# A hand-written order table of 1781 steps is replaced by another one: a recurrent attention layer and a gated two-layer network on one core

## The chip, the cores and the metric

The kernel runs on one core of a Trainium2 chip. The metric is the time of one execution on the device in microseconds (us), taken as the median over runs. The core has five engines with instruction queues of their own: TensorE (PE) for matrix products, VectorE (DVE), ScalarE (ACT) and GpSimd (POOL) for elementwise work, and SyncE (SP), which here only issues transfers between the chip's memory and the core. Each engine takes its queue strictly in order, so an instruction that waits holds up all that stand behind it on the same engine.

## The reference

Two layers follow each other. The first is a recurrence over 768 time steps with a state matrix of 48 x 48 for each of 4 batches and 8 heads; the second takes its 3072 outputs of 384 numbers through a network of 384, 2048 and 384 columns.

```python
for t in range(S):
    cur = np.einsum('bhd,bhe->bhde', u[None] * kt, vt)
    y[:, :, t] = np.einsum('bhd,bhde->bhe', rt, state + cur)
    state = wt[:, :, :, None] * state + np.einsum('bhd,bhe->bhde', kt, vt)
...
h = x @ w_in
relu6 = np.clip(h + 3.0, 0.0, 6.0)
g = h * relu6 / 6.0
return (g @ w_out).astype(np.float32)
```

The weights of the second layer come as 64-bit floats, the rest as 32-bit floats.

## The kernel before

**Tiling.** The sequence is cut into 24 chunks of 128 steps. For a chunk DVE scans the decays backward and forward (`back_scan` L430, `fore_scan` L439), scales k and r (L450, L454, and from chunk 7 on POOL does that), and PE makes scores, transposes k, writes to the state and reads from it (L500, L516, L600, L578, L587). Four chunks make a block of 512 tokens, and there are six blocks. In block 0 the second layer is done plainly: `up` (L716), a ramp on ACT, `gate` on DVE (L727), `down` (L735). In blocks 1 to 5 both products are done with fewer multiplications: sums of the inputs (`sum_x`, L778 to L782) feed 40 products (`up_product`, L831, 2 halves of 20 with 2 matmuls each), DVE and ACT read the results (`up_read`, L839 to L848), then come ramp and gate (L852, L856), sums of the gated values (`sum_g`, L871), and 28 products a block for the output (`down_product`, L886), read out by ACT and DVE (L902, L904) and stored by SP (`store`, L746).

**Start.** The weights must be turned from 64-bit to 32-bit floats before block 0 can use them. A pair of weight tiles is fetched by SP (`fetch`, L393, 768 KB into a `bits` buffer), ACT makes two passes over it (`low_whole` L402 and `high_sign` L407), DVE shifts and adds (`high_shift` L413 and `high_low` L417). There are 16 such pairs. PE, while it has nothing to do in the first 60 us, runs small products whose result nobody reads (L1262, here called fillers).

**End.** Besides the result the kernel checks that its inputs allow the short way of computing: 38 reductions of re-read inputs on DVE (`vet`, L932 and L935), eight small instructions that join them (`verdict`, L945 to L955), a product of one column on PE (`count`, L959), and a copy of the number into `flag` on DVE (L962). Behind the kernel's last step every engine loads that flag into a register (L1535) and branches over a second, general version of the kernel when it is zero (L1536).

**What sets the order.** The kernel is written as 1781 named steps, each with its engine, its predecessors and the buffers that it holds (rings: four PSUM banks called `bank`, one called `bankS`, one `y`, three `bits` buffers and so on). The table `ORDER` gives each step a rank, two characters a step, and the steps are written out in this rank. That is then the order on every engine. Since a step takes the buffer that came free earliest in this order, the table also decides which buffer, and so which reader, a step waits for. The fillers too are put in by the kernel's own times for the steps, so their number at each place follows the order.

```python
rank = [CODE.index(ORDER[2 * i]) * 64 + CODE.index(ORDER[2 * i + 1]) for i in range(len(steps))]
out = [n for _, n in sorted(zip(rank, steps))]
```

Of the kernel before, what the change touches and what calls it, by code (L numbers as in the profile page):

```python
# [81 lines left out]
ORDER = (
    "AAADAIAQAKAOALANAPARASAYAVAjATAXAZAdAmAqAfAoAzA3A/ACAFAWAiAcAnAbAaAeAgAhAlAtAyAkApAxA1A5A9A8A+BNBUBcAJAMBIBfBSBaBRBF"
    "BJBTBVBXCGCLBpBvCBCRBdCYCdCnCyC7AUAvBjB4BuCABzBeBgBlBmBqCSCaCJCOCWCrCNCuC1E0DCDMDVDgBOBQCpC2DcDkCvCUCbCiDDDXDuDyC+DH"
    "DjFFDKFMFQFUFfFnFwCXDLC9DGEOEZDBDADRDWDsEKFzDZDqFPFWE5FZFeFkF3GVGXGlGfCcC4D9EJFmFpEEDYDwD+F2F5GYFlFvFoGNGPGSGiG0G5Do"
    "FxETFyF+GDEXEDFXFcGhGjG6F7GdF8GrGzG2HPHYHkH0HsEdGaF4GZGxG1F9FdGWGgHAHCHcGnHHGoHMHOHRH/IEIIFrG8FuGkG7HXHhGqGcGpHbHeIJ"
    "HVHiHWHyH2H9IrJWJlJtJ0GHHdGIG/HmItIyHGGtHNIPIVJcIDINIHIYIcKMLfLkG3IKG9HzILI/JCH3HZHjJeJjLnIvJbIwJgJiLxMAMLMWMQHnJdHo"
    "JvJ4K/LDJ1IBIdLqLuMIKTLtLwL1MRMfMmI4LlI6KHLmL6MBKOJUJnMFMPMpL4MJMbMiMwOvO9PEPLLHMGLKLrMHMZMeLyLZL0MtMxO5MYMrL9MvMzM6"
    "PJP+QKLSMnLVMNMoNANHMUL2MTO2PIQCM4O8M3PoPpPsQWQdQiQyQqNYO4NaOSO3PXPbOYN5OFQBQGQjPPQJPQQNQQQXQ5RIRQOCQEOEPhQDQcQgPlOg"
    "PRQrQwRUQbQvQeQxQ0Q1R3SoS1S6TCOHQkOKQIQlRERLQSPUQMRZRcSwQ+RWRARgRjRnTlUdUlRNRRRVRqRwSISNRvR/SOSuS9UiR7SzR8ULUNUPUvU9"  # L90
    "VOVUVYSCSvSETATWT+UCTISeSpUqUtVDTsUhTqUnUpUuVWVhVqSUUkSXTgUjU8VATkSyTGVCVKVsU1VHU6VLVPVVWAYTYVYjYZShVESnUrVFVbVfUxTL"
    "UyVxV2YWVaVoVdVzV3YdYgYnUGVpUHVMVrWFWLVTU0VQYbYfYqWEYaWIYcYhYtYwYyY5Y1BCABAEArAuAsA2AGA4A7AwBAAHBDBHA6BPBBB1B+B7CFCD"
    "ClCoCmCwA0CTCZBrChBLCHCKCQC6CVC0C5DNDSD8EhEmEfEsDPDzD2D1EcCgD/EBDQEkCsDfDiDpDtEpE/FCE+FgEGErEvEwE2E1FKFOFLFVDvE3E6En"
    "FABGBMBWB3B8B/EUEbEiBZBhBtBkBxB0FaFhFiBbBiBoBnCCCPEAEIELBEBKBYBsByB2EHEPERB6CECIEeEoEuBwB5B9ExFIFRCMCeCjENESEWCfCtCz"
    "EQEVEYC3C/DEFSFYFbC8DIDOElEtEyCkCxDFD0D7ECCqDbDhEaEgEjDJDTDaG+HKHQDUDeDmE4E9FDDlDxD3EqEzE7DdDnDrD5EFEME8FBFHFjFtF0F6"
    "F/GCGEGBGFGKGMGRGbGeGmGuGvGsGwGyG4HBHJHUHaHrH6HgHlHqHwH1H5ICIGITIXD4D6FEFGFJFNFTFqGOGQGTGUHDHEHFHIHLHSHTHfHpHtHuHvHx"
    "H4H7H8H+IAIRIUIWIaIgIhIjIkIlInJNJPFsF1GAGGGJGLKDKhIFIOIpI5IeIuI2JGJqI+JAJLIQISI7IMIiImIZIzJDJOJRJkIqI0IxIbI8IsI9JEIo"
    "IfJYJQI3JBJIJVJXJpJ5KBKFJZKAJTJrJFJKJwJzJ6J9JMJSI1JHJ7KIKdKkKrJaJfKuJ+KEKXJmJxKGJuJ2KCKUKSKaJ/KRKKJsKiKJKYKqJ3JyKoKz"
    "J8KcKLKjKVKmKxK0K4KZKeK5K9KfKlKsKvKpKtKwK1KPKbKNLOLMLULCLGLLLYKnLAK2LELILNLQLTLWLaLbLjL3L5LFLJLXLRLcLpL8LdL+LeLhLvMC"
    "LgLiL/MMKgKyLoLsK7K8L7MDMKMOMXMaMlM9K3LzMSLBMVMgNCMdNEMkMsMyM+NQNVNeNpNyNsNuN4MqNBNgMuM5NIM1NKNSNmNZNkNTNbNXM0NhNMNd"  # L100
    "NzNDM7NtN9NPNoNWNxNfN1N6OUOuNjNnOOOXNrNvNwN3N7OPN2OJNcNiOBOLOWOlOtObOeOnN0N8OTN/OGOQNFNOOiO1OqO6OIOROMODOdOVOZOjONNJ"
    "OoOrOcOhOmO7O0PAPFPMPSPGPKOxO+OkOpOsOwPDPHOzPBOaOfOyPnPNPuPZPdPkPyO/PVPCPcPiPmPqPtPwP0P2P5QAQHPgPjPxPrP6P/QRP8QTP3P9"
    "QUQfP4P7QZQsPOPTQLQPPYPaQaQhQoQzQtQ2Q9RDPWQYQpPfQ3Q6RGQ7RHRBRPRYRdRbRmRuR6SGRORTSDRyR1SARFRXRhReRrSKSdSgStRkRsR5RKRz"
    "RpRtR0RfRlSBSHRxSFSWSiSlS0S3S5S+SqSsSQSVSfS7ScSmTDTJR2SMR+SZS8THTPTfTpS/TETxS2S4TYSJSYSPSSSkSxTRTKTVTBTNTMSLTUSTTbTr"
    "SjSaTjT2SrTdTFTXTQTZT0T3T7TSTnT5T8ThTmToTuTcTeTvTyTOTTTwT4UIUTUBUFUMUWTiUAT9UDUJUOUQUSUUUXUYUgUsU2UEUKUVURUZUoU5UbU7"
    "UaUeUwU3UcUfU/VSTaTtUmU4T1T6UzVBVIVcVNVRVZVnTzU+VJT/ViVXVvVlVyVkVuV1V6WDWKWpWyW8XdXgXrVtVwWTV0V+WGV4WPWeWlWmWtWHWRWN"
    "V5WuWMWUXlWBV9W2XxWXWdWjWwWoWxXEXIXMWqWsX1X3WgWiW5W+W0W4XoXsWSWVW1W/XUXbXjX2X5YDWbWhXGV7WWWYWnWvW3XCXNXXW7XFXAWOXYWc"
    "XKX7WZWrXeYHWzXLW9XaXRXcXnXqXvXTXVYIYKXOXSXhXkXfXiX8X+XDXHYeYmYsY0YkYoYvY4X6YLYlYrYQYUYxYzY2Y8Y6Y7Y/ZKYOYuY3YYZAY9ZN"
    "ZDZPW6XBXPX4XpXwX0YFXQXmXJXuX/YAXyYBX9YXYGYJYNYPXtXzYEYCYiYMYRYpYSY+ZBZFZIZRZVZZZcZ2ZEZHZqadakasZCZLZaZJZOZXZmZiZtZU"
    "ZYanZGZbZdZfZkZQZMZhZuZSayZeZrZnZxZ8Z+aBZsZwZyZ3a1a9ZlZpZ4Z7ZoZ0aparZTZgaMaYamaCaJaQahaoazZzZ/Z9ZvZ6aKaUaSabZWZjauZ5"  # L110
    "aRaAaDaLaEZ1acaTaHa5aOaaaWagaqatawaZaeaVaXa+bCafaiajalaNaPaxa8aFaIa2bEa0a4bAbLaGa3ava6bDbFa/bIbGbMbSbXbabca7bBbKbHbO"
    "bZbebQbfbPbUbbbhbRbVbkbpbJbNbYbgbWbibdblbnbsbqbrbubxbTbjbobmbvbtbzbwb0JJJhK+LPJoKQKWK6MjNGMEMcMhM8M2NNNqN+NLOANlM/NU"
    "NRPePzPvP1QOQFQmQ/Q8QVQnQuRCRaRiQ4RMRJRSR9R4RoSbSRVjV8V/VGVgVeVmWJWQWCWaWfWkXWXZby"
)
# [1490 lines left out]
```

## Time and profile before

| | before |
|---|---|
| median of 3 runs (lowest, highest) | 545.09 us (544.74, 546.12) |
| span of the profiled execution | 544.0 us; no own time is listed for it; the median of the runs lies 1.1 us above this span |
| instructions in the trace | 13407 |
| PE busy | 532.9 us, 98% of the span |
| DVE busy | 425.1 us, 78% |
| ACT busy | 268.1 us, 49% |
| POOL busy | 112.9 us, 21% |
| read from memory, written | 59.90 MB, 4.72 MB |

The span runs from the first to the last instruction of one execution. "Busy" is the time in which an engine works on an instruction; waiting, branches and the issue of transfers are not counted. The ends of matmuls are modelled, so a short wait of PE can be hidden in its busy time. In the trace a 32-bit matmul counts as two instructions, so the counts of PE are twice those of the program.

### The profile page before, as it was taken

What the parts mean: (1) busy time and instruction counts of PE and PEld (TensorE: products, weight loads), DVE (VectorE), ACT (ScalarE), POOL (GpSimd) and SP (SyncE); (2) the same over time, 40 slices, a digit from 0 to 9 for tenths busy, and PEclk for the clock granted to TensorE, in tenths of its full rate; (3) what the DMA queues carried; (4) which work ended last, traced back from release to release, by engine and by line L of the source; (5) the groups of instructions that cost most, each with busy time, mean ns of one, the idle gap of its engine ahead of it and who ended that gap; (6) DMA issues with size and microseconds to landing.
All of it is one profiled execution on the core that took longest, in us unless ns stands there. A gap on an engine that the chain in (4) does not pass through costs nothing.

```text
span 544.0 us, 13407 instructions
## 1 busy us (share of the span) xinstructions
PE 532.9 (98%) x5558; PEld 466.7 (86%) x5558; DVE 425.1 (78%) x726; ACT 268.1 (49%) x657; POOL 112.9 (21%) x111
## 2 busy tenths in 40 slices
...
PEclk9999999999999999999999999999999999999998
...
GB/s 302 364 152 336 259 176 105 126 118 126 65 170 82 77 188 110 222 187 177 23 147 153 288 203 162 0 118 87 170 58 1 2 16 31 30 0 2 1 29 36
DMA packets 29686, 66.66 MB, mean 123 GB/s; under 512 B 3216, under 2 KB 10544, under 8 KB 29616
## 3 DMA queue, kind: packets, MB, share of 16 engines
...
q14 instruction: 24, 0.20, 0.1%
q10 hardware_dynamic: 128, 0.00, 0.0%
HBM read 59.90 MB, written 4.72 MB: 119 GB/s over the span
## 4 chain that ended last, share of the span: by engine, by line
PE 87%; DVE 7%; DMA 2%; issue 1%; ACT 1%; DVEq 0%; ACTq 0%
PE bank L886 28%; PE bank L831 22%; PE bank L735 7%; PE bank L716 7%; PE bankS L886 5%; PE bankS L831 4%; DVE g L848 3%; PE y_ps L578 2%; PE y_ps L600 2%; PE bank L500 2%; PE ps L516 2%; PE y_ps L587 2%; DVE g L856 1%; DMA bits<-in_moe_w_out_dram 1%; PE bankS L1262 1%
## 5 line engine op out<-in xcount | busy, mean ns | idle before, releaser
L852 ACT ACTIVATE clip<-g,three 128x512 f32<-128x512 f32 x80 | 56.9, 721 | 55.3 <-DVE g L848 45.9
L848 DVE TENSOR_TENSOR g<-bank,g 128x512 f32<-128x512 f32 x80 | 53.6, 684 | 10.1 <-PE bank L831 8.6
L856 DVE SCALAR_TENSOR_TENSOR g<-clip,g 128x512 f32<-128x512 f32 x80 | 56.2, 716 | 5.8 <-ACT clip L852 5.8
L886 PE MATMUL bank<-w_out,g 128*128 128x192 f32 x320 | 57.3, 327 | 0.0
L491 ACT ACTIVATE A<-eyes,dg 128x64 f32<-128x64 f32 x192 | 49.5, 338 | 11.0 <-PE y_ps L587 10.7
L886 PEld LDWEIGHTS bank<-w_out,g 128*128 128x128 f32 x320 | 52.8, 190 | 1.2 <-DVE g L856 0.3
L450 POOL TENSOR_TENSOR K<-feat_in,E 112x512 f32<-112x512 f32 x17 | 23.1, 1361 | 133.8 <-PE bank L500 128.0
L716 PE MATMUL bank<-xT,w_in 128*128 128x256 f32 (+1 forms) x216 | 45.5, 362 | 0.7 <-issue 0.7
L683 ACT COPY xT<-y_ps 48x256 f32<-48x256 f32 x88 | 32.2, 366 | 27.7 <-PE y_ps L587 26.9
L735 PE MATMUL bank<-w_out,g 128*128 128x384 f32 x128 | 43.8, 491 | 0.0
L716 PEld LDWEIGHTS bank<-xT,w_in 128*128 128x128 f32 x216 | 36.5, 190 | 5.3 <-issue 0.9
L831 PE MATMUL bank<-xT,w_in 128*128 128x256 f32 x160 | 40.5, 381 | 0.4 <-DVE g L848 0.4
L846 ACT COPY g<-bank 128x512 f32<-128x512 f32 x50 | 28.8, 582 | 20.7 <-PE bank L831 17.2
L735 PEld LDWEIGHTS bank<-w_out,g 128*128 128x128 f32 x128 | 23.5, 190 | 14.2
L831 PEld LDWEIGHTS bank<-xT,w_in 128*128 128x128 f32 x160 | 30.0, 190 | 5.2 <-DVE g L848 0.8
L902 ACT ACTIVATE o<-bank 128x192 f32<-128x192 f32 x30 | 9.9, 330 | 49.7 <-PE bank L886 49.6
L430 DVE TENSOR_TENSOR_SCAN E<-feat_in,back 112x520 f32<-112x520 f32 x24 | 31.5, 1312 | 2.2 <-DMA feat_in<-in_feat_dram 1.1
L454 POOL TENSOR_TENSOR W<-feat_in,W 112x512 f32<-112x512 f32 x17 | 22.8, 1342 | 44.3 <-DVE W L439 44.3
L439 DVE TENSOR_TENSOR_SCAN W<-feat_in,start 112x520 f32<-112x520 f32 x24 | 31.4, 1308 | 0.6 <-PE y_ps L578 0.4
L507 DVE COPY_PREDICATED A<-mask,bank 128x256 f32<-128x256 uint8 x48 | 18.6, 441 | 16.3 <-PE bank L500 16.1
L831 PE MATMUL bank<-xT,bits 128*128 128x256 f32 x120 | 30.9, 381 | 0.0
L886 PE MATMUL bank<-more,g 128*128 128x192 f32 x160 | 28.7, 328 | 0.0
...
## 6 DMA issues: line engine op xcount, KB each, us to landing
...
```

What stands on the lines that cost most here:

```text
L430: nc.vector.tensor_tensor_scan(out=E_[:, ::-1], data0=d["w"][:, :0:-1], data1=back.rearrange("q p t -> q (p t)")[:, ::-1], initial=0.0, op ...
L439: nc.vector.tensor_tensor_scan(out=W_, data0=d["w"][:, :-1], data1=starts[i % 2].rearrange("q p t -> q (p t)"), initial=0.0, op0=ALU.mult, ...
L491: nc.scalar.activation(out=d["A"][:, h, :], in_=eyes, func=ACT.Copy, scale=d["dg"][:, h])
L683: nc.scalar.copy(out=blocks[bk]["xT"][g * GP:g * GP + D, :, at:at + HL], in_=st[i]["y_ps"][a][(g ^ a) * GP:(g ^ a) * GP + D, :, :])
L716: nc.tensor.matmul(h_ps[:, :(c1 - c0) * L], lhsT=w_in[:, f // 2, j, f % 2, :], rhs=b["xT"][:, j, c0 * L:c1 * L], start=(j == 0), stop=(j = ...
L735: nc.tensor.matmul(b["o", c][:, :DM], lhsT=g_of(0, f, c), rhs=w_out[:, f, :], start=(f == 0), stop=(f == NFC - 1))
L831: nc.tensor.matmul(b["p", d, c][:, z * HB:(z + 1) * HB], lhsT=weight(W_PLACE[r], d)[:, z, :], rhs=x_at(bk, X_PLACE[r]), start=fresh and z ...
L846: nc.scalar.copy(out=out_, in_=src)
L848: nc.vector.tensor_tensor(out=out_, in0=src, in1=out_of(bk, d, other), op=ALU.add if sign > 0 else ALU.subtract)
L852: nc.scalar.activation(out=c, in_=out_of(bk, d, u), func=ACT.Relu, bias=three, scale=twice)
L856: nc.vector.scalar_tensor_tensor(out=g, in0=blocks[bk]["r", d, u], scalar=6.0, in1=g, op0=ALU.min, op1=ALU.mult)
L886: nc.tensor.matmul(b["d", p, to][:, :h], lhsT=a, rhs=w(), start=(f == 0 and k in (1, 5)), stop=(f == HF - 1 and k in (2, 3, 4)), skip_grou ...
```

## The change

Only the text of `ORDER` differs. The table was searched anew under three sets of step times instead of one: as traced, with transfers and hand-overs between engines delayed, and with early transfers. The steps, their engines, predecessors and buffers are the same 1781, so the amount of work is the same. The number of fillers is 38 in both. Of the diff a line or two show the kind of thing:

```diff
-    "AAADAIAQAKAOALANAPARASAYAVAjATAXAZAdAmAqAfAoAzA3A/ACAFAWAiAcAnAbAaAeAgAhAlAtAyAkApAxA1A5A9A8A+BNBUBcAJAMBIBfBSBaBRBF"
+    "ADAWAGALAJAPAHAKANAOARAaAbAiASATAYAcAhArAkAvAzA7A+AMAgAQAeAdAqAVAUAZAmAnAuA2A6ApAtA3A4A/BKA9BBBIBOBZAfBtAwBCBECEA1Ay"
```

What it does to the order is shown at four places.

**SP and DVE at the start.** `feat_in` is a chunk's r, k and decays, `v_in` its v, `bits` a raw weight pair. SP before:

```order
L348 DMA feat_in<-in_feat_dram 128x521
L356 DMA feat_in<-in_feat_dram 128x2x512
L351 DMA feat_in<-in_feat_dram 128x3x521
L363 DMA v_in<-in_tok_dram 128x384
L393 DMA bits<-in_moe_w_in_dram 128x3x256
```

SP now:

```order
L393 DMA bits<-in_moe_w_in_dram 128x3x256
L348 DMA feat_in<-in_feat_dram 128x521
L356 DMA feat_in<-in_feat_dram 128x2x512
L351 DMA feat_in<-in_feat_dram 128x3x521
L363 DMA v_in<-in_tok_dram 128x384
```

A weight pair is now fetched ahead of the first chunk's decays. On DVE, where `E` and `W` are the scans' results and `rk` is r times k, before:

```order
L430 SCALAR_TENSOR_TENSOR E<-feat_in,back 112x520
L434 RECIPROCAL start_79<-E 112x8
L439 SCALAR_TENSOR_TENSOR W<-feat_in,start_79 112x520
L463 TENSOR_TENSOR rk<-feat_in 112x512
L454 TENSOR_TENSOR W<-feat_in,W 112x8x64
```

DVE now, behind the same memsets:

```order
L413 TENSOR_SCALAR top<-bits 128x768
L430 SCALAR_TENSOR_TENSOR E<-feat_in,back 112x520
L434 RECIPROCAL start_79<-E 112x8
L417 ISA w_in<-top,more 128x1536
L439 SCALAR_TENSOR_TENSOR W<-feat_in,start_79 112x520
L463 TENSOR_TENSOR rk<-feat_in 112x512
```

The conversion of that pair (L413 and L417) moves in front of and between the first chunk's scans. ACT's two passes of the same pair now stand at the head of its queue, ahead of the small transfer of `u_col` that ACT issues itself. ACT before:

```order
L349 DMA u_col<-in_ug_dram 112x8
L457 ACT_TABLE_LOAD
L457 COPY w_min<-E 112x8
L481 COPY dg<-ps 128x8
```

ACT now:

```order
L402 ACT_TABLE_LOAD
L402 ACTIVATE more<-bits 128x768
L407 ACTIVATE more<-bits 128x768
L349 DMA u_col<-in_ug_dram 112x8
L457 COPY w_min<-E 112x8
```

The transfer of `u_col` is issued behind two conversions that wait for the weight pair; PE needs `u_col` for its first real product (L475).

**PE from the first read of chunk 0 on.** The rows start behind that read (L578, L587), the first score (L500) and the write (L600) of chunk 1. Before:

```order
L1262 MATMUL bankS<-ident 128x128 x3
L659 MATMUL y_ps<-xT,S__115 128x64 x6
L651 MATMUL bank<-xT,ident 128x256 x2
L578 MATMUL bank<-W,S 48x64 x8
L587 MATMUL bank<-A,v_in 48x64 x16
L716 MATMUL bank<-xT,w_in 128x128 x6
L475 MATMUL ps<-u_col,rk 64x2 x8
L1262 MATMUL bankS<-ident 128x128 x6
L659 MATMUL bank<-xT,S__115 128x64 x6
```

Now:

```order
L659 MATMUL y_ps<-xT,S__115 128x64 x6
L651 MATMUL bank<-xT,ident 128x256 x2
L578 MATMUL bank<-W,S 48x64 x8
L587 MATMUL bank<-A,v_in 48x64 x16
L475 MATMUL ps<-u_col,rk 64x2 x8
L716 MATMUL bank<-xT,w_in 128x128 x6
L659 MATMUL bank<-xT,S__115 128x64 x6
L1262 MATMUL bankS<-ident 128x128
L716 MATMUL bank<-xT,w_in 128x128 x3
```

Behind the first L578 of chunk 0 there stood 10 fillers, and now there are 3; ahead of it there stood 28, and now there are 35. The real products ahead of it are the same set in both.

**PE in block 1, behind the read of chunk 9.** The rows begin with the last score of chunk 10 (numbers tell buffers apart; a `bank` number that did not occur above is a bank newly taken). Before:

```order
L500 MATMUL bank_2106<-W_2013,K_1801 64x64
L831 MATMUL bank_2127<-xT_1343,apart_88 128x256 x2
L831 MATMUL bank_2127<-xT_1343,bits_1178 128x256 x2
L831 MATMUL bankS_2058<-T__1913,w_in_85 128x256 x2
L831 MATMUL bank_2156<-T__1913,bits_1178 128x256 x2
```

Now:

```order
L500 MATMUL bank_2070<-W_1894,K_1768 64x64
L831 MATMUL bank_1962<-xT_1309,bits_1317 128x256 x2
L831 MATMUL bank_2102<-T__1837,bits_1211 128x256 x2
L831 MATMUL bank_2109<-T__1837,w_in_85 128x256 x2
L831 MATMUL bankS_2023<-T__1837,w_in_85 128x256 x2
```

Before, the first product after the score takes a bank anew and so needs DVE or ACT to have read the one before it; now it goes on in bank 1962, which is open since before the read of chunk 9.

**DVE and SP at the end.** `o` is the output of a chunk, `flag` the number that all engines load. The last rows of DVE before:

```order
L871 TENSOR_TENSOR S__5300<-S__5300,g_5070 128x512
L871 TENSOR_TENSOR S__5300<-g_5070,S__5300 128x512
L904 SCALAR_TENSOR_TENSOR o<-bank,o 128x192 x2
L1535 TENSOR_LOAD flag
L1536 COMPARE_AND_BRANCH
```

DVE now:

```order
L904 SCALAR_TENSOR_TENSOR o<-bank,o 128x192
L945 TENSOR_REDUCE beyond<-w_max 128x1
L946 TENSOR_SCALAR bad<-beyond 128x1
L947 TENSOR_REDUCE low<-w_min 112x1
L949 SCALAR_TENSOR_TENSOR bad<-low,bad 112x1
L952 TENSOR_REDUCE beyond<-word_max 128x1
L953 SCALAR_TENSOR_TENSOR bad<-beyond,bad 128x1
L954 TENSOR_REDUCE beyond<-word_min 128x1
L955 SCALAR_TENSOR_TENSOR bad<-beyond,bad 128x1
L904 SCALAR_TENSOR_TENSOR o<-bank,o 128x192
L962 CAST flag<-ps 1x1
L1535 TENSOR_LOAD flag
```

The verdict is formed between the last two outputs and the flag is written behind them; `count` on PE (L959) moves behind PE's last output product. SP before loaded the flag with eight stores still to come, in the rows

```order
L926 DMA feat_in<-in_moe_w_out_dram 128x768
L1535 TENSOR_LOAD flag
L1535 ISA x2
L746 DMA out_dram<-o 128x384
L690 DMA xT<-xT 16x256 x6
```

and now it does so behind all of them:

```order
L926 DMA feat_in<-in_moe_w_out_dram 128x768
L746 DMA out_dram<-o 128x384 x4
L1535 TENSOR_LOAD flag
L1535 ISA x2
L1536 COMPARE_AND_BRANCH
```

So the flag load and the branch that hangs on it move, on every engine, behind the end of the last product.

More of the change, by code (lines that the diff above doesn't have):

```diff
@@ L82 @@
 ORDER = (
-    "AAADAIAQAKAOALANAPARASAYAVAjATAXAZAdAmAqAfAoAzA3A/ACAFAWAiAcAnAbAaAeAgAhAlAtAyAkApAxA1A5A9A8A+BNBUBcAJAMBIBfBSBaBRBF"
-    "BJBTBVBXCGCLBpBvCBCRBdCYCdCnCyC7AUAvBjB4BuCABzBeBgBlBmBqCSCaCJCOCWCrCNCuC1E0DCDMDVDgBOBQCpC2DcDkCvCUCbCiDDDXDuDyC+DH"
-    "DjFFDKFMFQFUFfFnFwCXDLC9DGEOEZDBDADRDWDsEKFzDZDqFPFWE5FZFeFkF3GVGXGlGfCcC4D9EJFmFpEEDYDwD+F2F5GYFlFvFoGNGPGSGiG0G5Do"
-    "FxETFyF+GDEXEDFXFcGhGjG6F7GdF8GrGzG2HPHYHkH0HsEdGaF4GZGxG1F9FdGWGgHAHCHcGnHHGoHMHOHRH/IEIIFrG8FuGkG7HXHhGqGcGpHbHeIJ"
@@ L87 @@
[L87 to L111, printed above, removed]
@@ L112 @@
-    "bZbebQbfbPbUbbbhbRbVbkbpbJbNbYbgbWbibdblbnbsbqbrbubxbTbjbobmbvbtbzbwb0JJJhK+LPJoKQKWK6MjNGMEMcMhM8M2NNNqN+NLOANlM/NU"
-    "NRPePzPvP1QOQFQmQ/Q8QVQnQuRCRaRiQ4RMRJRSR9R4RoSbSRVjV8V/VGVgVeVmWJWQWCWaWfWkXWXZby"
+    "ADAWAGALAJAPAHAKANAOARAaAbAiASATAYAcAhArAkAvAzA7A+AMAgAQAeAdAqAVAUAZAmAnAuA2A6ApAtA3A4A/BKA9BBBIBOBZAfBtAwBCBECEA1Ay"
+    "BDBQBjB6CUCXBoBzB9CDBhCICMCPCdCpAsBWBYB0BnCHBmBTBXBiCGCTCrCsB+CFCJCRBwChCmDLC1DDDgDhBvCVCeC3DKDVCkCQCcCoCyDUDeDmC8DI"
+    "DfDqCuD4ETEZE9FTFdCWDzDTD1D6ESDjC5DPDvDyEnFlECEFEfEzDlE+FEFGF6GJGiHSGlCfEuELE6FQF4EbDxEPEXFjF1GhFMFcFSFfFtGCGkG5HEEd"
@@ new lines @@
+    "FYE8FoGBGLFOEoExE7GbGeHHF+GXGKGpGsGzHQHXHjHvHxFZGWFyGaGvG2F0F3GMGcHCHlHmG1HFG3HGHNHaHrH2IKGPHBGZGmHDHZHnGxG4HLHoH+IA"
+    "HVHkHfH6H9IRIuJBJSKXKSGVHpGYHKHeH5H8HYHgIOIlIoJIHwIbIMJPJUKeLTLXHAIBITHiH7I/JEHtJtKFKMK+LcI0KKJKKtLELjLuLwL+L1IPJ3Jr"
+    "IfJTLGLZI6KVK/LaLmL5KpLeL3L8MKMRM+KLLhKRK8LYLrL4LALPLpL/MJMULlMIMTMZNVOYOxQbP4LbL0LyLqMHMPMaMCMGMpNAOVOdMLMeMbMqNwOp"
+    "PAPpPuMYNPMuMxNNNiNtM8NRPFPNPdPwNgO0OwPaPiP6P9QQQRQvQuNZPGNxN9O3PQPTOWPjP5QFQMQkPeP7PSQIQNQYQnRBRYPfQJP/PsP3QTQjPyQW"
+    "QlQ0Q3RHQOQgQVQyQ6RKRqSSSsTdTeQAQrQoQBQcQwQ7QCRCReR8SPSXQ9RSRcRrSgS3TVUNUWQaRVQhRRRlRxTARhRkRtSqS7URSGTJS/T5T9UPUbUs"
@@ new lines @@
+    "UuVHVMRTTfSQSFTFT4UKSjSnTyUiUxVETkUVUBUdUfU1U/VLWYTbUrTgTiUQUjU7UCUJUqVJVKVXUnU+U3VQVVVwWoXmXuYoYnULU4UgUYU2VRWyUkU6"
+    "U9XDXFXxVBWPVZXWXfYBYTYZUmVSVOVCV/XoYOVnVgVvX4YEYaW2XwWxX/YNYbYcYgYvYwFWAEAXAlA0AxBAAAABACAFAIAjA5BGBFBHAoBJBSBNBsCK"
+    "CZCiCgCnA8BlBuB1B8BVCOClCvC2CSC4C7CwDCCqDQDZDSDwEAEWEiEGEtD0EBEID3EUDADYDsDdD+E4FKFLFCFbEkEwE5FAFnFXFeFrFmFwEcEjElEq"
+    "EvBLBPBRBfBqBxF5GdGwBMBbBgBeB2B3ErFBFJBpByB5B7B/CCEEEOERBUBcBdBaBkBrEyE0FDCYCaCjEgEmE1B4CBCLEYEhEsCACNCbEKEVEaC9DJDO"
+    "D7D/EHCzC6C+FiFzF7DaDnDtEDEJEQCxDBDGDpDuD5CtC0C/FFFNFUDEDMDNFpFsF2DFDRDbE3FHFIDHDXDcDoDrD2DWDiDkD8D9EMEeE2FRFaFhF8F9"
```

18 lines of the change are left out of this document (added).

## The prediction

> **What bounds the kernel now.** I read the page first: which engine fills the span, and at which clock.
>
> ```profile
> span 544.0 us, 13407 instructions
> PE 532.9 (98%) x5558; PEld 466.7 (86%) x5558; DVE 425.1 (78%) x726; ACT 268.1 (49%) x657; POOL 112.9 (21%) x111
> PEclk9999999999999999999999999999999999999998
> ```
>
> PE is the bound, at full clock throughout. Since the work is the same 1781 steps, the change can only move what PE does not need: the time before its first useful product, the fillers, its waits, and the tail behind its last product. How these spread over the span shows the view by stretches (columns: stretch, its length, then busy time of PE, weight loads, DVE, ACT and POOL, clock, share of the transfer engines, GB/s).
>
> ```profile
> 0.00:14.50 14.50, 12.68 (x164) 11.74 (x164) 12.02 (x23) 7.12 (x24) 3.01 (x15) 1.00 0.88 306
> 14.50:26.00 11.50, 10.57 (x227) 9.46 (x226) 9.64 (x19) 10.14 (x26) 0.00 (x0) 1.00 1.03 365
> 26.00:465.00 439.00, 436.65 (x4778) 377.80 (x4778) 365.16 (x621) 227.28 (x566) 109.92 (x96) 1.00 0.39 129
> 465.00:538.00 73.00, 72.98 (x395) 67.73 (x393) 38.27 (x66) 23.25 (x42) 0.00 (x0) 1.00 0.04 15
> 538.00:544.00 6.00, 0.00 (x0) 0.00 (x0) 0.00 (x0) 0.33 (x1) 0.00 (x0) 0.69 0.13 44
> ```
>
> From 26 to 538 us PE idles only 439.00 - 436.65 + 73.00 - 72.98 = 2.4 us. Behind it lie 6 us in which no engine computes. So there is little to win in the middle, and the two ends are as large as it. Next the waits of PE and of its weight loads (engine, line, what was waited for, us in total, times, longest).
>
> ```profile
> PE bank L831 <- DVE g L848: 0.8, 2, 0.5
> PE bank L716 <- issue: 0.7, 1, 0.7
> PE y_ps L600 <- ACT kvs L611: 0.4, 1, 0.4
> PEld bank L831 <- ACT g L846: 2.8, 12, 0.5
> PEld bank L831 <- DVE g L848: 1.9, 3, 0.8
> PEld y_ps L600 <- ACT kn L521: 1.1, 2, 0.5
> PEld bank L831 <- ACT bankS L839: 1.0, 3, 0.5
> ```
>
> Most are products of blocks 1 to 5 that need a bank, or a partner, that DVE or ACT has only just read. Two of them in the timeline (start, duration):
>
> ```profile
> 156.38 0.91 PE L831 MATMUL bank<-xT,apart 128*128 128x256 f32 x3 [0.46 <-DVE g L848]
> 252.30 1.03 PE L831 MATMUL bank<-xT,bits 128*128 128x256 f32 x4
> 253.68 0.73 PEld L831 LDWEIGHTS bank<-xT,w_in 128*128 128x128 f32 x4 [0.76 <-DVE g L848]
> 254.81 0.86 PE bankS L831 x4
> ```
>
> A product step takes 0.86 us when nothing holds it (last row, from the chain of waits). At 252.30 the next starts 1.38 us later, so 0.52 us was lost, of which the busy column hides 0.16, because it lets the step before end after 1.03.
>
> **The start, step by step.** These rows give what stands between the first transfer and PE's first read of chunk 0.
>
> ```profile
> 3.80 1.31 DVE L430 TENSOR_TENSOR_SCAN E<-feat_in,back 112x520 f32<-112x520 f32 x1 [1.07 <-DMA feat_in<-in_feat_dram]
> 9.96 0.65 DVE L463 TENSOR_TENSOR rk<-feat_in 112x512 f32<-112x512 f32 x1
> 11.37 0.64 PE L475 MATMUL ps<-u_col,rk 112*64 112x2 f32 x16
> 14.50 0.65 PE L578 MATMUL y_ps<-W,S 48*48 48x64 f32 x16
> 24.26 1.60 PE L1262 MATMUL bankS<-ident 128*128 128x128 f32 x12
> 25.70 1.45 PE L659 MATMUL bank<-xT,S__115 112*128 112x64 f32 x12
> ```
>
> ```profile
> L417 DVE CUSTOM_DVE_ANT_0 w_in<-top,more 128x1536 uint16<-128x1536 uint16 x8 | 7.6, 951 | 0.7 <-ACT more L407 0.6
> L402 ACT ACTIVATE more<-bits x16: 1062/1086/1126, 14.6 to 80.1; 128x768 uint16<-128x768 uint32 x16
> L407 ACT ACTIVATE more<-bits x16: 1043/1066/1084, 15.5 to 81.0; 128x768 bf16<-128x768 int32 x16
> u_col<-in_ug_dram ACTq DMA_DIRECT2D x1, 3.5 KB, 3.1
> ```
>
> *The weight pair ahead of the decays.* It is 768 KB, 0.786 MB; at the 365 GB/s of the second stretch 2.1 us, so the first scan starts at 5.9 instead of 3.80. DVE's shift of the pair falls into that wait and costs nothing. The joining step L417 stands between the scans and adds 0.95. It needs ACT's two passes, 1.09 + 1.07 behind a landing at about 5.1, so 7.3, when scan and reciprocal end at 7.5: hidden, by 0.2. The second rk product (9.96, ends 10.61) thus ends 3.05 later, at 13.7, and its PE product follows at about 13.8 instead of 11.37: 2.4 later, since before it stood behind fillers. From there PE needs in the new order about as long to the first read as the 3.1 us of before (a score more, four fillers fewer), so that read slips by 2.4. Bounds: 1.0, when the pair's transfer runs beside that of the decays and only L417 bites, and 3.05, when all of it reaches PE.
>
> *Fillers.* Seven move from behind this read to ahead of it. Six take 25.70 - 24.26 = 1.44 us, so seven give back 1.7. This is real time only if the products behind them are ready; conversions done early are what makes them ready. If not, the fillers turn into waits, bound 0.
>
> *The idle 0.7 at L716 "issue".* Nothing in the trace says what it was; half of it, 0.35, I count as gone, bounds 0 and 0.7.
>
> Start in sum: 2.4 - 1.7 - 0.35 = +0.35.
>
> **The middle.** Steps that were late by a few tenths now find other products ahead of them, as behind the read of chunk 9, where PE goes on in an open bank. Lower bound of what can go: the 2.4 us of idle. Upper bound: the four rows of weight loads, 6.8 us in 20 waits, less the 0.13 (0.86 - 0.73) that each contains in ordinary running: 4.2. I take 3.5: the 2.4, and for some seven waits of over 0.15 the hidden 0.16 each. For new waits of the same kind I add 0.4, with 0 and 2.4 as bounds (that the new order waits as much as the old). Sum: -3.1.
>
> Reductions moved late (L935) run on DVE, which is busy 38.27 of 73.00 us in the last stretch: no cost, as long as the last two outputs do not wait for them. The eight small verdict instructions stand ahead of the last but one output; that store then leaves about 1.5 us later and is still ahead of the last. In blocks 1 and 2, where they stood before, they free DVE a little; that is part of the 3.5.
>
> **The tail.** Behind PE's last product the flag must still be formed, loaded and branched on.
>
> ```profile
> 419.39 0.19 PE L959 MATMUL ps<-ones,bad 128*1 128x1 f32 x2
> L962 DVE CAST flag<-ps x1: 140/140/140, 419.7 to 419.7; 1x1 int32<-1x1 f32 x1
> L1535 SPq TENSOR_LOAD <-flag x1: 475/475/475, 419.8 to 419.8; - x1
> L1535 SPq FUSED_REGOPS  x1: 191/191/191, 420.4 to 420.4; - x1
> L1536 POOLq COMPARE_BRANCH  x1: 45/45/45, 450.4 to 450.4; - x1
> L1536 POOLq EVENT_SEMAPHORE  x1: 17/17/17, 453.1 to 453.1; - x1
> L1536 ACTq COMPARE_BRANCH  x1: 50/50/50, 538.6 to 538.6; - x1
> L1536 ACTq EVENT_SEMAPHORE  x1: 17/17/17, 542.5 to 542.5; - x1
> L1536 SPq COMPARE_BRANCH  x1: 45/45/45, 538.8 to 538.8; - x1
> L1536 SPq EVENT_SEMAPHORE  x8: 17/17/17, 542.0 to 542.6; - x8
> ```
>
> From the count on PE to SP's load went 0.4 us; the last store's issue on SP covers that. But load and register work, 0.48 + 0.19 = 0.7, were hidden at 419.8 and now stand between the last store and SP's branch at 538.8. Behind a branch the next instruction comes only after 2.7 us (POOL alone, 450.4 to 453.1), 3.2 (SP) and 3.9 (ACT, at the same time as SP). Now all five engines branch together. For that I add 0.3, between 0 (SP's 3.2 stays) and 2.1 (a second engine raised 2.7 to a mean of 3.5, or 0.7; three more at that rate). Sum of the tail: +1.0.
>
> [...]
>
> **Sum.** +0.35 - 3.1 + 1.0 = -1.75 against the profiled span of 544.0, so 542.25. The median lies 1.1 above that span, so 543.3.
>
> **Rivals.** *All waits go and the tail stays cheap* (chance 0.15): start -0.35 (the whole idle 0.7 gone), middle -4.2, tail +0.7: 541.2. For it speaks that most waits are of tenths and a little distance removes them; against it that new ones always come with a new order.
>
> *The tail, or new waits, eat the gain* (0.18): five fetches at once, +2.1 instead of 0.3, give 545.1; so does a middle that keeps 1.8 us of waits. For it speaks ACT's 3.9 beside SP's 3.2; it decides from 1.5 us of tail beyond the forecast.
>
> *The late u_col* (0.07), the one that makes it slower: PE's first real product needs `u_col`, which ACT now issues after its first passes, at 6.2 to 7.3, instead of 0.8. With the 3.1 us of its row it lands at 9.3 to 10.4, when that product is due at 10.3. Behind the queue of large transfers that then runs (share 1.03 in the second stretch) it could take as long as they do. Each us beyond 10.3 delays everything on PE; from 13.7 on the kernel is slower than before by over 0.3%; at 15 it is 548. Against it speaks that it landed in 3.1 us at the start too, with SP's transfers beside it. [...]
>
> **Chances and range.** My forecast with its smaller deviations has 0.60, two thirds of it below 543.45, which is 0.3% under 545.09 (about what a measurement of this kernel tells from no change). Faster: 0.40 + 0.15 = 0.55; the same: 0.20 + 0.18 = 0.38; slower: 0.07. The range reaches from the first rival, 541.0, to 0.6 above the second, 545.7; it leaves out the third, and about as much below.
>
> **What would show it.** In the profile after: the first scan at 5.9 and the first read of chunk 0 near 16.9 (start term); PE idle from 26 us to its end below 1 us, and no wait of 0.3 us on L831 (middle); PE's last product ending near 535; SP's branch 1.5 us behind it instead of 0.8, and the next instruction 3.2 to 4 us behind that (tail). The prediction is wrong if the first read stands beyond 18.5, if PE waits in the middle as long as before, or if the last branch takes over 5 us.

## The result and the profile after

The changed kernel takes 548.34 us (median of 11 runs, 547.27 to 552.49) against 544.98 us before: ratio 1.007, 95% interval 1.0055 to 1.0086. It is slower by 3.4 us. The forecast was faster by 1.8 us, with 545.7 as its upper end.

The runs of the changed kernel differ among themselves by the granted clock: 552.0 and 552.5 us with a mean clock of 0.985 over the span, 549.0 to 549.5 at 0.989 and 0.990, and 547.3, 547.3 and 547.6 in the three runs at 0.998. The profiled execution is one at 0.985, with 552.0 us and a span of 550.0. Its page:

```profile
span 550.0 us, 13376 instructions
PE 536.3 (98%) x5558; PEld 473.7 (86%) x5558; DVE 432.3 (79%) x726; ACT 264.8 (48%) x657; POOL 107.3 (20%) x111
PEclk9599999999999999999999999999999999999998
```

The second slice, 13.75 to 27.5 us, has clock 5 instead of 9. That is new. The view by stretches (columns as before: length, PE, weight loads, DVE, ACT, POOL, clock, transfer share, GB/s) puts limits to it:

```profile
8.90:11.20 2.30, 0.01 (x1) 0.00 (x0) 2.30 (x5) 0.00 (x0) 0.00 (x0) 1.00 1.07 377
11.30:24.80 13.50, 13.32 (x162) 12.10 (x166) 8.57 (x15) 6.83 (x23) 0.00 (x0) 0.50 0.71 262
26.00:465.00 439.00, 435.86 (x4869) 379.26 (x4869) 368.60 (x611) 231.00 (x584) 104.28 (x96) 1.00 0.40 129
465.00:543.40 78.40, 78.40 (x432) 74.00 (x430) 48.04 (x87) 22.56 (x44) 0.00 (x0) 1.00 0.11 37
543.40:550.00 6.60, 0.06 (x2) 0.00 (x0) 0.15 (x1) 0.31 (x1) 0.00 (x0) 0.78 0.14 45
```

PE is idle from 8.9 to 11.4 us, and from 11.24 to 24.89 (the clock's own records) it works at half speed, although it is busy nearly all the time: 162 instructions in 13.5 us, where the kernel before did 250 in the same stretch:

```profile
11.30:24.80 13.50, 12.57 (x250) 11.16 (x249) 11.64 (x24) 11.69 (x31) 0.00 (x0) 1.00 1.04 372
```

The timeline of the start shows what PE waited for:

```profile
1.43 7.49 PE L1262 MATMUL bankS<-ident 128*128 128x128 f32 x52 [1.43 <-POOL ident masks.py:199]
5.63 0.38 ACTq L349 DMA_DIRECT2D u_col<-in_ug_dram  x1
6.61 1.24 DVE L430 TENSOR_TENSOR_SCAN E<-feat_in,back 112x520 f32<-112x520 f32 x1 [0.42 <-DMA feat_in<-in_feat_dram]
8.00 0.91 DVE L417 CUSTOM_DVE_ANT_0 w_in<-top,more 128x1536 uint16<-128x1536 uint16 x1
9.98 0.67 DVE L463 TENSOR_TENSOR rk<-feat_in 112x512 f32<-112x512 f32 x1
11.39 1.02 PE L475 MATMUL ps<-u_col,rk 112*64 112x2 f32 x16 [2.47 <-DVE K L450]
17.43 1.02 PE L475 MATMUL ps<-u_col,rk 112*64 112x2 f32 x16
23.07 1.09 PE L578 MATMUL y_ps<-W,S 48*48 48x64 f32 x16
```

and the list of transfers how long u_col took (issues, size, us to landing):

```profile
u_col<-in_ug_dram ACTq DMA_DIRECT2D x1, 3.5 KB, 5.6
```

The fillers end at 8.92. The first product needs rk, which ends at 10.65, and u_col, which was issued at 5.63 and took 5.6 us: it landed at 11.25. The profile names DVE's K as releaser, but K happens to end at 11.25 too, and the product does not read it (two runs below tell the two apart). The first read of chunk 0 comes at 23.07 instead of 14.50. The waits of PE in the whole span:

```profile
PE ps L475 <- DVE K L450: 2.5, 1, 2.5
PE bankS L1262 <- POOL ident masks.py:199: 1.4, 1, 1.4
PE bank L831 <- DVE T__3513 L778: 1.3, 1, 1.3
PE bank L831 <- DVE A L507: 0.8, 1, 0.8
```

Where before several waits of up to 0.5 us stood in the middle, there are now two large ones, both at L831. From 26 to 465 us PE now idles 439.00 - 435.86 = 3.1 us, where it was 2.35 before and less than 1 had been forecast. The tail: PE's last output product in the timeline, and the rows of the flag's load and branch (duration in ns, first and last start):

```profile
540.58 2.76 PE L886 MATMUL bank<-more,g 128*128 128x192 f32 x16
```

```profile
L1535 SPq TENSOR_LOAD <-flag x1: 521/521/521, 544.1 to 544.1; - x1
L1536 SPq COMPARE_BRANCH  x1: 45/45/45, 545.0 to 545.0; - x1
L1536 PEldq COMPARE_BRANCH  x1: 4318/4318/4318, 544.3 to 544.3; - x1
L1536 SPq EVENT_SEMAPHORE  x8: 17/17/17, 548.1 to 548.6; - x8
```

SP's branch stands 1.7 us behind the end of PE's last product (543.34) instead of 0.8 (538.8, with PE's last product ending at 537.98), and SP goes on 3.1 us later, as against 3.2 before.

Cut at the first read of chunk 0 and at the end of PE's last product, the difference of the two profiled executions is: start 23.07 - 14.50 = +8.6; middle (543.34 - 23.07) - (537.98 - 14.50) = 520.3 - 523.5 = -3.2; tail 6.6 - 6.0 = +0.7. The sum is +6.0, as the spans say. The forecast in the same cut was +2.4, -5.15 and +1.0.

### The profile page after: what moved, and what is told of

It is laid out like the page before. It is cut to its first block, busy times and chain, and to the rows that moved or that the text cites. A ratio compares the mean times of both kernels' runs of the same rounds, so it can differ in the third digit from the quotient of the medians.

```text
span 550.0 us, 13376 instructions
## 1 busy us (share of the span) xinstructions
PE 536.3 (98%) x5558; PEld 473.7 (86%) x5558; DVE 432.3 (79%) x726; ACT 264.8 (48%) x657; POOL 107.3 (20%) x111
## 4 chain that ended last, share of the span: by engine, by line
PE 90%; DVE 5%; issue 1%; ACT 1%; DVEq 0%
PE bank L886 27%; PE bank L831 26%; PE bank L735 8%; PE bank L716 7%; PE bankS L886 5%; PE bankS L831 5%; PE y_ps L578 2%; PE bank L500 2%; PE y_ps L600 2%; PE ps L516 2%; PE y_ps L587 2%; PE ps L475 1%; PE bankS L1262 1%; DVE T__3513 L778 1%; DVE W L439 0%
## 5 line engine op out<-in xcount | busy, mean ns | idle before, releaser
L856 DVE SCALAR_TENSOR_TENSOR g<-clip,g 128x512 f32<-128x512 f32 x80 | 58.4, 748 | 2.0 <-ACT clip L852 2.0
L831 PE MATMUL bank<-xT,w_in 128*128 128x256 f32 x160 | 40.9, 379 | 0.0
L439 DVE TENSOR_TENSOR_SCAN W<-feat_in,start 112x520 f32<-112x520 f32 x24 | 32.8, 1365 | 3.7 <-PE y_ps L578 3.7
L831 PEld LDWEIGHTS bank<-xT,w_in 128*128 128x128 f32 x160 | 30.3, 190 | 3.9
L430 DVE TENSOR_TENSOR_SCAN E<-feat_in,back 112x520 f32<-112x520 f32 x24 | 29.9, 1246 | 3.7 <-POOL K L450 3.2
L454 POOL TENSOR_TENSOR W<-feat_in,W 112x512 f32<-112x512 f32 x17 | 24.4, 1433 | 43.2 <-DVE W L439 43.2
L831 PE MATMUL bank<-xT,bits 128*128 128x256 f32 x120 | 30.7, 380 | 0.0
L886 PE MATMUL bankS<-w_out,g 128*128 128x192 f32 x160 | 28.6, 326 | 0.0
L904 DVE SCALAR_TENSOR_TENSOR o<-bank,o 128x192 f32<-128x192 f32 x20 | 7.1, 353 | 26.6 <-PE bank L886 17.7
```

What stands on the lines that cost most here:

```text
L430: nc.vector.tensor_tensor_scan(out=E_[:, ::-1], data0=d["w"][:, :0:-1], data1=back.rearrange("q p t -> q (p t)")[:, ::-1], initial=0.0, op ...
L439: nc.vector.tensor_tensor_scan(out=W_, data0=d["w"][:, :-1], data1=starts[i % 2].rearrange("q p t -> q (p t)"), initial=0.0, op0=ALU.mult, ...
L831: nc.tensor.matmul(b["p", d, c][:, z * HB:(z + 1) * HB], lhsT=weight(W_PLACE[r], d)[:, z, :], rhs=x_at(bk, X_PLACE[r]), start=fresh and z ...
L856: nc.vector.scalar_tensor_tensor(out=g, in0=blocks[bk]["r", d, u], scalar=6.0, in1=g, op0=ALU.min, op1=ALU.mult)
L886: nc.tensor.matmul(b["d", p, to][:, :h], lhsT=a, rhs=w(), start=(f == 0 and k in (1, 5)), stop=(f == HF - 1 and k in (2, 3, 4)), skip_grou ...
```

## The experiments

Two theories stood against each other. *Clock*: the idle time ahead of PE's first product makes the granted clock fall, and the work behind it then runs at half speed. *Late start*: the start is simply late, and the clock is a side matter. Besides these, the tail and the two waits in the middle had to be priced. Where code is inserted, line numbers shift by 1 to 3.

### Closing the gap with fillers

```diff
+ for _ in range(11 if n == "dot0" else 0):
+     self.spin()
```

> The changed order with 11 more fillers ahead of PE's first product (37 instead of 26), so that PE stays busy until u_col and rk are there; nothing else is moved. Theory 'clock': in the changed kernel PE idles 2.5 us from 8.9 us on and then runs at half clock for 13.7 us; without the idle time the granted clock stays at 1.00 in the first 30 us and at 0.997 or 0.998 over the span in every run, the first read of chunk 0 comes at about 17 to 18 us instead of 23.07, and the time falls to 547.4, where the four runs of the changed kernel at clock 0.998 stand. Theory 'late start': the idle time itself is what costs; then nothing changes, 548.3 with the same spread of clocks.

Measured: 547.11 us (546.69 to 547.20), ratio 1.0038 (1.0024 to 1.0053). The clock held in the stretch from 11.2 us (columns as above):

```profile
11.20:16.00 4.80, 4.80 (x105) 4.47 (x107) 4.57 (x8) 3.40 (x13) 0.00 (x0) 1.00 1.06 390
```

The first read of chunk 0 came at 18.25 instead of 23.07, and the spread over the runs shrank from 5 us to 0.5. So the idle time is what lowered the clock here; useless work in its place saves 4.8 us at that read and 1.2 in the median. (At a mean clock of 0.998 stand three runs of the changed kernel, not four as said in the expectation.) The rest of the loss, 2.4 us, remains though the clock held.

### u_col first

```diff
  def constants():
+     nc.scalar.dma_start(out=u_col, in_=ug)
...
- nc.scalar.dma_start(out=u_col, in_=ug)      # load_feat(0)
```

> The changed order with the small transfer of u_col issued first on ACT, as in the kernel before; nothing else is moved. Theory 'u_col': its landing at 11.25 us, not DVE's K that the profile names, released PE's first product at 11.39; with u_col landed by 6 us that product starts at about 10.75, right behind rk (end 10.65), PE idles 1.8 us instead of 2.5, and the time falls by 0.6 us where the clock does not fall, by more where the shorter idle time keeps the clock up: 546.7 to 547.7. Theory 'K': PE waited for DVE's K (end 11.25); then the first product stays at 11.4 and the time at 548.3.

Measured: 546.58 us (546.05 to 548.39), ratio 1.0036 (1.0023 to 1.0049), a little under the 546.7 to 547.7 expected.

```profile
6.44 1.24 DVE L430 TENSOR_TENSOR_SCAN E<-feat_in,back 112x520 f32<-112x520 f32 x1 [0.33 <-DMA feat_in<-in_feat_dram]
10.40 0.69 DVE L450 TENSOR_TENSOR K<-feat_in,E 112x512 f32<-112x512 f32 x1
10.54 0.63 PE L475 MATMUL ps<-u_col,rk 112*64 112x2 f32 x16 [1.14 <-DVE rk L463]
16.96 0.65 PE L578 MATMUL y_ps<-W,S 48*48 48x64 f32 x16
```

PE's first product starts 0.85 us earlier, released by rk. K ends only at 11.09 here, behind the start of that product: so it waited for u_col and not for K. With 1.1 us of idle time the clock held in this execution, and the first read of chunk 0 came at 16.96: the 16.9 of the forecast. Of the other seven runs 548.39 us stands apart, and one of 547.12 us has a mean clock of 0.993 where the rest have 0.996 to 0.998, so the clock may have fallen there. With the start as forecast and the clock held the time is still 3.3 us above the forecast of 543.3: that part of the miss lies behind the first read.

### A gap in the kernel before

```diff
+ made = 0
  while now < self.start[n] - 0.12:
-     self.spin()
+     if n != "dot0" or made < 4:
+         self.spin()
+         made += 1
```

> The kernel before with 9 of the 17 opening fillers left out, so that PE idles about 2.5 us (4.7 to 7.26) ahead of its first product; the order is untouched. Theory 'clock': the granted clock falls to 0.50 for a stretch of some us to 14 us in some of the runs, each us at half clock costs about half a us, and the time spreads from 545 to 551 with a median of 546 to 549. Theory 'late start': the fillers only pass the time; 545.0 as before, clock 0.997.

Measured: 549.91 us (545.17 to 550.68), ratio 1.0078 (1.0051 to 1.0105); a median of 546 to 549 had been expected. With the old order and nine fillers fewer the kernel before is as slow as the changed one:

```profile
7.13 1.02 PE L478 MATMUL ps<-u_col,rk 112*64 112x2 f32 x16 [1.91 <-DVE rk L466]
20.23 0.98 PE L581 MATMUL y_ps<-W,S 48*48 48x64 f32 x16
25.89 0.65 PE L581 MATMUL bank<-W,S 48*48 48x64 f32 x16
```

```profile
14.00:21.00 7.00, 7.00 (x52) 6.17 (x51) 2.17 (x5) 4.00 (x13) 0.00 (x0) 1.00 0.71 263
```

The product at 7.13 takes 1.02 us, the same in the prediction's rows 0.64. The reads of chunks 0 and 1, of the same size, take 0.98 at 20.23 and 0.65 at 25.89; the first record of the clock in this trace is a rise at 20.96, so up to there full speed had not been granted. That differs in form from the changed kernel, where the clock rose at 4.42 and fell again, but the price is of the same kind: the first read of chunk 0 comes 5.9 us later than the 14.36 of the kernel before in e5_before. The clock row (the last but two of the columns, here from 14 to 21 us) reads 1.00 ahead of the rise, since the trace holds only changes; the durations of equal products tell the truth.

### The early flag

The three steps `verdict`, `count` and `flag` go ahead of the last two outputs, the rest of the changed order stays. The edit is a change in the text of `ORDER`; here and below it is written with the names of the steps.

```diff
+ verdict before out5.1.u;  count before down5.1.7.1;  flag before out5.1.c22
```

> The changed order with verdict, count and flag moved ahead of the last two outputs, so that the flag is ready some 5 us before PE's last product; nothing else is moved. Theory 'five branches at the end': PE, DVE and POOL load the flag and branch ahead of ACT and SP again; SP's branch stands 0.8 us behind PE's last product instead of 1.7, and what lies outside the span goes from 1.95 back to 1.1 us: 1.5 us in all, 546.8 (the clock at the start is as in the changed kernel). Theory 'only the load': five branches together cost nothing more; SP's load and register work, 0.7 us, is all that goes: 547.6.

Measured: 546.76 us (546.64 to 547.23), ratio 1.0036 (1.0022 to 1.0051). From PE's last product to the end it takes 5.57 us instead of 6.64:

```profile
L1536 PEldq COMPARE_BRANCH  x1: 3846/3846/3846, 536.8 to 536.8; - x1
L1536 SPq COMPARE_BRANCH  x1: 45/45/45, 540.1 to 540.1; - x1
L1536 SPq EVENT_SEMAPHORE  x8: 17/17/17, 542.9 to 543.5; - x8
```

PE's last product ends at 539.27, so SP's branch follows after 0.8 us. Time less span stayed at 1.8 us; that part of the expectation was wrong. The clock fell in this execution too, for 3.4 us, so the time mixes both, and its agreement with the expected 546.8 proves nothing; the tail's price is read from the two traces, 1.1 us, one execution each. This trace also names what PE's first product waits for, which the profile of the changed kernel put down to K:

```profile
PE ps L475 <- DMA u_col<-in_ug_dram: 1.9, 1, 1.9
```

### The kernel before, once more

> The kernel before once more, unchanged, to see its own time, span and clock side by side. Theory 'outside is the same': time less span is 1.7 to 2.0 us as in all later runs, so the span of 544.0 shown for the kernel before belonged to an execution at about 545.8, above the median; this run shows 544.7 with a span of about 543, ratio 1.000. Theory 'outside grew': time less span is 1.1 us here, and the changed kernel's 1.9 us is a cost of its own.

Measured: 544.79 us (543.03 to 546.93), ratio 0.9987 (0.9975 to 1.0000), the profiled execution 543.94 us with a span of 542.2. Time less span is 1.7 us. So the span of 544.0 belonged to an execution of about 545.7, not to the median. The middle of that kernel differs from one execution to the next as well (above the row of this execution, whose counterpart in the prediction has PE at 436.65):

```profile
26.00:465.00 439.00, 437.62 (x4782) 379.13 (x4782) 365.25 (x626) 226.85 (x565) 110.38 (x96) 1.00 0.39 130
```

Here PE idles 1.4 us in 439 instead of 2.35.

### The late flag alone

```diff
  (the order before)
+ verdict before out5.1.c12;  count behind end;  flag before store5.3
```

> The kernel before with verdict, count and flag alone moved to the end, as the changed order has them. Theory 'late flag': the stretch from PE's last product to the end of the span grows from 6.0 to 6.6 to 7.0 us, since all five engines load and branch together: 545.3 to 545.7, ratio 1.001 to 1.002. Theory 'hidden': the last store's landing covers it, 544.7.

Measured: 545.61 us (544.32 to 546.69), ratio 1.0009 (0.9996 to 1.0022). The stretch behind PE's last product took 6.68 us, against 5.98 and 6.24 in the two executions of the kernel before. By the times, 545.61 where 545.3 to 545.7 had been expected, this is not told from nothing.

### The old start before the changed rest

The first 360 steps stand in the old order (up to chunk 4's read, at 86 us), the others in the changed one.

> The first 360 steps in the order of the kernel before (up to chunk 4's read, 86 us), the rest in the changed order. Theory 'start': the start is what makes the changed kernel slower; with the old start the first read of chunk 0 is back at 14.5, the clock stays up, PE's last product ends at about 537.2, and with the late flag the time is 544.3 to 545.0, as before. Theory 'middle': the changed order loses behind 86 us too (its waits of 1.3 and 0.8 us for DVE at L831); then PE ends as late as in the changed kernel without its clock loss, 538 to 539, and the time is 546 or more.

Measured: 546.22 us (545.37 to 547.78), ratio 1.0018 (1.0007 to 1.0029). The first read of chunk 0 is back at 14.38 and the clock holds, which takes the ratio from 1.007 to 1.0018: most of the loss is in the start. But 1.0018 is neither of the two expectations in full. PE's last product ends at 537.39, against 537.98 and 535.98 in the two executions of the kernel before: it is not shown that the changed order loses behind 86 us, and no gain of it shows there either.

### Old start and early flag

> As the last one (old start up to chunk 4's read, changed order behind it), with verdict, count and flag ahead of the last two outputs as well. Theory 'start and tail': what is left is the changed order's gain in the middle; PE's last product ends at 537.2, the tail falls to 5.6 us, and the time is 543.3 to 544.1, faster than the kernel before by 0.6 to 1.4 us. Theory 'middle': 545 or more.

Measured: 544.82 us (543.95 to 546.09), ratio 0.9993 (0.9982 to 1.0004), between the two expectations: the time of the kernel before. With start and tail taken out, what is left of the changed order is worth 0.4 us, between a gain of 1.0 and a loss of 0.2. The two waits at L831 are all there (1.3 and 0.7 us), and the timeline of DVE and POOL shows what the sums met:

```profile
297.69 0.35 DVE L537 TENSOR_TENSOR S<-S,kvs 112x192 f32<-112x192 f32 x1
297.96 0.42 DVE L778 SCALAR_TENSOR_TENSOR T__3513<-xT 128x256 f32<-128x256 f32 x1
298.12 0.62 POOL L529 TENSOR_TENSOR S<-S,w_min 112x192 f32<-112x192 f32 x1 [5.51 <-DVE S L537]
298.41 1.75 DVE L778 SCALAR_TENSOR_TENSOR T__3513<-xT,T__3513 128x256 f32<-128x256 f32 x1
298.70 1.18 POOL L454 TENSOR_TENSOR W<-feat_in,W 112x512 f32<-112x512 f32 x1
299.85 1.18 POOL L466 TENSOR_TENSOR rk<-rk_in 128x384 f32<-128x384 f32 x1
300.20 1.10 DVE L780 TENSOR_TENSOR T__3513<-T__3513,xT 128x256 f32<-128x256 f32 x1
```

A sum that starts ahead of POOL takes 0.42 us, those behind it 1.75 and 1.10; the rows of the next experiment show the very same sums at 0.42. POOL had waited 5.5 us for DVE's L537 (the step mid17), which the changed order puts right ahead of the sums: DVE wakes the engine that then stands in its way.

### POOL woken later

`mid17` goes behind the sum tx3.0, `mid21` behind tx4.1; else as the last one.

```diff
- ... mid17, ..., tx3.0, diag117, ...        - ... mid21, fore22, ..., tx4.1, decb21
+ ... tx3.0, mid17, diag117, ...             + ... fore22, ..., tx4.1, mid21, decb21
```

> As e8_both (old start up to chunk 4's read, changed order behind it, early flag), and two DVE instructions moved: the product of L537 that releases POOL's next work, mid17 and mid21, goes behind the sums of L778 to L782 that stood behind it (tx3.0, tx4.1). Theory 'POOL and DVE exclude each other': in e8_both the sums of L778 and L780 took 1.75, 1.10 and 1.10 us instead of 0.42 while POOL ran, and PE waited 1.3 and 0.7 us for them at L831; with POOL started later they take 0.42 each, both waits are gone and the time falls by 1.5 to 2.0 us, to 543.0 or so. Theory 'another wait': the products behind need something else as late; the waits only change their name, 544.5 to 545.0.

Measured: 543.26 us (542.28 to 543.80), ratio 0.9968 (0.9957 to 0.9978): faster than both kernels.

```profile
297.75 0.42 DVE L778 SCALAR_TENSOR_TENSOR T__3512<-xT,T__3512 128x256 f32<-128x256 f32 x1
298.21 0.42 DVE L780 TENSOR_TENSOR T__3512<-T__3512,xT 128x256 f32<-128x256 f32 x1
299.44 0.51 POOL L529 TENSOR_TENSOR S<-S,w_min 112x192 f32<-112x192 f32 x1 [7.22 <-DVE S L537]
302.35 1.11 DVE L782 TENSOR_TENSOR T__3512<-T__3512 128x256 f32<-128x256 f32 x1
```

What is left among PE's waits there:

```profile
PE bank L831 <- DVE T__3512 L780: 0.9, 1, 0.9
```

The sums run in 0.42 us each while POOL is still asleep, and the two waits at L831 are replaced by one of 0.9, for a sum that now meets POOL at 302.35. (The second of the two was for DVE's read L507, which stood behind sums that POOL's work had stretched to 1.1 and 1.2 us.) PE ends 1.9 us earlier than in e8_both, but the execution shown is the fastest of the twelve; by the ratios the two moved steps are worth 1.4 us. This is the largest gain found in the middle, and it is two steps of 1781.

### The changed order with its three repairs, and with the gap closed

> The whole changed order, its start included, with the three local repairs: u_col's transfer first on ACT, verdict, count and flag ahead of the last two outputs, and mid17 and mid21 behind the sums. Theory 'the parts add up': from the 544.4 span of the run with u_col first go 2.0 us of waits at L831 and 1.0 us of tail: span 541.4, time 543.3, faster than the kernel before by 0.3%. Theory 'late start': the late start of the changed order can't be won back and the time stays at 545 or above.

Measured: 544.87 us (544.12 to 554.65), ratio 1.0001 (0.9979 to 1.0024), where 543.3 had been expected. Two of twelve runs took 550.9 and 554.7. In the profiled execution PE idled 1.58 us ahead of its first product, and the clock fell for 3.4 us:

```profile
10.47 0.63 PE L475 MATMUL ps<-u_col,rk 112*64 112x2 f32 x16 [1.58 <-DVE rk L463]
```

```profile
11.20:16.00 4.80, 4.80 (x67) 4.61 (x67) 4.07 (x6) 3.20 (x13) 0.00 (x0) 0.64 1.05 389
```

The mean clock of 0.64 over 4.8 us is half speed for 3.4. The last kernel closes the gap:

```diff
+ for _ in range(7 if n == "dot0" else 0):
+     self.spin()
```

> As e10_repaired (the whole changed order with u_col first, the early flag and the two moved products), and 7 more fillers ahead of PE's first product (33 instead of 26), which close the 1.6 us in which PE idled there. Theory 'clock': what spread e10_repaired from 544.1 to 554.7 and took 3.4 us at half clock in its profile was this idle time; now the clock holds in every run, the first read of chunk 0 comes at about 17.0 us instead of 18.53, and the time is 543.0 to 543.6 with no run above 545: as fast as e9_ports, faster than the kernel before. Theory 'late start': the spread has another source and the time stays at 544.9.

Measured: 544.56 us (543.89 to 545.44), ratio 0.9986 (0.9975 to 0.9997). No run lies above 545.5, and the clock held in the profiled execution. That fits the theory that the gap made the outliers; two of twelve against none of twelve does not prove it. The median misses the 543.0 to 543.6 expected. In the profiled execution the fillers ended only at 11.5, since the clock rose at 6.66 instead of 4.4 and they had run longer at half speed; the first product followed at 11.47 and the first read of chunk 0 at 17.89. The same number of fillers is long or short according to when the clock rises: the 26 of e10_repaired took 7.46 us with the rise at 4.38, the 26 of e4_tail 8.13 with the rise at 5.79.

## Why the prediction was wrong

Two steps failed: the start, which had no term for the clock, and the middle, whose gain of 3.1 us did not come. Of the 5.0 us between forecast and median the middle is the larger part: e2_u, with the start as forecast and the clock held, is still 3.3 us above the forecast.

**The start** (forecast first read 16.9, measured 23.07). Three terms of it were worked out: the pair ahead of the decays, L417 between the scans, and the fillers. The first two hold in sum: where u_col was first and the clock held, the read came at 16.96. Singly they do not, and that the sum fits is luck: the first scan came at 6.44 instead of 5.9, and from there to the second rk product the order needed only 0.4 us more than before (6.55 against 6.16), where 0.95 was put down for L417.

What failed is the sentence on the fillers, which took them for time that is either real or a wait. Nothing in it asked how long PE stands idle between the last filler and the first product, nor what the idle time does. The answer, by the runs: at 2.5 us the clock fell for 13.7 us (changed kernel), at 1.9 and 1.6 us for 3.4 (e4_tail, e10_repaired), at 1.1 not in the execution profiled (e2_u), and without a gap it held in both profiled executions (e1_fill, e11_all). In all three traces with a fall it came 6.8 us behind the rise (4.42 to 11.24, 5.79 to 12.62, 4.38 to 11.21), and in the last 3.4 us ahead of it PE had idled 2.3, 1.9 and 1.6 us; in e2_u its whole gap was 1.1. At a clock of 0.50 half of 13.65 us is lost at most, 6.8 us by estimate; between the changed kernel and e1_fill the end of PE's last product differs by 5.2. In the two profiled executions of the kernel before PE idled 0.4 us there at most, and the clock held.

In the profiled executions the shortest gap with a fall was 1.6 us (e10_repaired), the longest without one 1.1 (e2_u). Behind the gap of 2.5 us the clock stayed at 0.50 for 13.65 us, about four times the 3.4 of the two short falls, although PE was busy for 13.3 of 13.5 us there. The same program had mean clocks from 0.985 to 0.998 in its eleven runs, so the loss differs from run to run; what sets the length of a fall no run shows.

**The rival of the late u_col** was right in its mechanism: landing at 11.25, where 9.3 to 10.4 had been forecast and 10.3 was due, it released the first product. Its own share is 0.85 us (11.39 against 10.54). That its 548 us meets the median is chance: it asked for a landing at 15. The assumption that the 3.1 us of the start would hold behind SP's large transfers was wrong: 5.6, and 5.7 in e1_fill and e4_tail.

**The middle** (forecast -3.1, with -1.7 and -0.35 of the start's terms -5.15 from the first read on; measured -3.2). At an undisturbed clock, e1_fill against the kernel before, it is (538.14 - 18.25) - (535.98 - 14.36) = -1.7 by e5_before and -3.6 by the first profile, whose middle is 1.9 us longer. The seven fillers that no longer stand there account for 1.7 of that by the prediction's price, so the gain of the waits is 0 to 1.9 us by single traces; the better measure is e8_both, where the start is the old one and the ratio leaves 0.4 us (a gain of 1.0 to a loss of 0.2) for the 3.1. The unexplained idle time, of which 0.35 us was counted as gone, turns up at another line where the clock holds: 0.3 us in e1_fill, 1.0 in e2_u (L587, "issue"). Two terms of the 3.1 failed. The old waits were sized from one execution with 2.4 us of idle PE, where another has 1.4 (both from 26 to 465 us). The new waits were put at 0.4 us: two of them measure 1.3 and 0.75, and e9_ports shows that they come from DVE's sums, which last longer while POOL works. The prediction had looked at DVE's busy share only. The rows have the very same sums (L778, L780) at 0.42 us with POOL idle and at 1.75 and 1.10 beside POOL's L454 and L466; by what the one engine holds up the other is not shown.

**The tail** (forecast +1.0). Its stretch measured 6.0 and 6.2 us in the kernel before, 6.6 to 7.2 in five executions with the late flag, 5.6 to 6.5 in five with the early one. The five with the late flag lie 0.9 us above the five with the early one in the mean, so the size was nearly right. SP's load and register work, 0.7, is uncovered, as forecast. The 0.3 for five branches together does not show: from SP's branch to its next instruction it takes 3.0 to 3.6 us in the executions with the late flag and 2.8 to 3.9 in those with the early one. That fetches fill this time, as the second rival has it, no run shows, and its 2.1 us for five branches did not come.

**The base**: the time of the kernel before does not lie 1.1 us above the span of the same execution but 1.7 to 1.9. The span shown came from an execution some 0.7 us slower than the median. In the sum this cancels, since 543.3 is the median less 1.75; it bears on the middle, whose waits were sized from that slower execution.

Together, e1_fill against e5_before, without the clock: start +3.9, middle -1.7, tail +0.8, in all the 2.9 us between their spans of 545.15 and 542.22. The clock adds from nothing to about 5 us a run, by the times of the changed kernel from 547.3 to 552.5; in the median it is 1.2.

What stays open: how long a gap is safe, since each length was seen in one or two traces; why the clock stays low for 3.4 us in one execution and for 13.65 in another; and what of the difference between e11_all and e9_ports (0.9986 against 0.9968) is the later start and what is chance.
